# A Fourier mixer and gated FFN on one core: the pair stage in lots of 256 tokens, with seven products in both layers

## The chip, the core and the metric

The kernel runs on one core of one Trainium2 chip. The metric is the device time of one execution in microseconds, the median of several runs. The engines are TensorE (PE in the profile; its weight loads are PEld), VectorE (DVE), ScalarE (ACT), GpSimd (POOL) and SyncE (SP), which here only issues DMAs. Each engine works through its own queue in order and waits on semaphores for the others.

## What is computed

```python
# x: 8 x 3008 x 256;  w_gate, w_val: 256 x 1536;  w_out: 1536 x 256;  all float32
X = np.fft.rfft(x, axis=1)
Y = X @ (w_r + 1j * w_i) + (b_r + 1j * b_i)      # real and imaginary part
Y = sign(Y) * max(abs(Y) - 0.01, 0)              # on each part
y = np.fft.irfft(Y, n=3008, axis=1).reshape(24064, 256)
gate = 1 / (1 + np.exp(-(y @ w_gate)))
out = (gate * (y @ w_val)) @ w_out
```

## The kernel before

A float32 operand is split in two parts, high and low (`float32r`): the high part is a rounded copy that ScalarE writes, the low part is what VectorE (or GpSimd) finds by subtracting it. A product of two split operands is three matmuls: high x high, high x low, low x high.

The first stage (about 1006 us of the span) does the Fourier transforms of all eight batches by matmuls, the mixing between them, and, woven between these, the FFN of the first 9 x 512 tokens (`ffn1`, `ffn2`). The mixed tokens beyond these are written to DRAM (`yd`). Beside it GpSimd forms sums and differences of weight tiles (`make_t`, `t1` to `t4`), stores them (`td`), and SyncE's queue loads them back near the end of the stage (`load_t`, `load_t1`). The hidden width of 1536 is NF = 12 tiles of 128; two tiles (f0, f1) make one of NH = 6 column pairs `fp`.

The second stage is the pair stage, on the remaining 19456 tokens: 19 pairs of two lots of HW = 512 tokens. In the first layer, for each `fp` and for each of i = 0 (gate) and i = 1 (value), a 2 x 2 block problem stands: two hidden tiles x two lots, summed over the two halves of the 256 channels. It is done with seven products instead of eight. The token-side operands are a11, a12, a21, a22 (a lot's half of the channels) and their sums s1 to s4, which GpSimd forms and ScalarE and its helpers split once per pair (`operand`, `split`, at the places of `PREP_AT`). The product list is

```
1: a11 b11   2: a12 b21   3: s4 b22   4: a22 t4   5: s1 t1   6: s2 t2   7: s3 t3
```

Each product is three matmuls 512 wide, all of them in line L714. `half(k)` issues one half step (one `fp`, one i): product 1 into PSUM bank a, 6 into b, 5 into c, 7 into d; ScalarE copies bank a to SBUF (u, L739), VectorE adds u + b (L743), + c (L745), + d (L747); then products 2, 3 and 4 are added on top in banks a, c and d, and VectorE adds u to c (L768) and d (L774). So the sums of products are formed in SBUF by VectorE. The gate's four results pass the sigmoid on ScalarE, the value's are multiplied by them (L753, L764, L779 on VectorE, L772 on GpSimd), and the four hidden blocks are split (`high` L661, `low` L665). `second(n, j)` is the second layer: plain, 2 lots x 2 output tiles x 3 matmuls for one hidden tile, 12 matmuls 512 wide (L689 to L691), added up in four banks over all 12 hidden tiles and then copied out by ScalarE (L671). It is issued one to two half steps behind the first layer. So one half step is 21 + 12 matmuls 512 wide, and there are 19 x 6 x 2 = 228 half steps. The stage's instruction order is written out by hand (`manual_schedule`): each engine runs its instructions in the order of these calls.

Of the kernel before, what the change touches and what calls it, by code (L numbers as in the profile page):

```python
# [25 lines left out]
NPL = 9  # L26
HW = 512
# [3 lines left out]
NCB, NTMP, NHP = 10, 9, 12  # L31
# [78 lines left out]
def tile_fft_mix_ffn(ctx: ExitStack, tc, x, w_r, w_i, b_r, b_i, w_one, w_out, mf, mi, mis, fa, fb, mf0, fa0, out):  # L110
# [334 lines left out]
    BEHIND = 3  # L445
# [133 lines left out]
    def make_t(fp, i):  # L579
# [4 lines left out]
        for k, f in enumerate((f0, f1)):  # L584
            g.tensor_add(b[:, k], w1h[:, f, i], w1l[:, f, i])
# [35 lines left out]
    def operand(p, name):  # L621

        y = held["y", p]
        a11, a21, a12, a22 = y[:, 0, 0], y[:, 0, 1], y[:, 1, 0], y[:, 1, 1]
        g = nc.gpsimd
        if name == "s1":
            held["s", p] = p4.tile([P, HW], F32, name="sop", bufs=1)
            g.tensor_add(held["s", p], a21, a22)
        elif name == "s2":
            g.tensor_sub(held["s", p], held["s", p], a11)  # L630
        elif name == "s3":
            g.tensor_sub(a21, a11, a21)
        elif name == "s4":
            g.tensor_sub(held["s", p], a12, held["s", p])
        held["op", p, name] = {"a11": a11, "a12": a12, "a22": a22, "s3": a21}.get(name, held.get(("s", p)))

    def split(p, name, sub_):
        v = held.pop(("op", p, name))
        t = p4.tile([P, 2, HW], F32R, tag="xop", bufs=NCB, name=name)
        nc.scalar.copy(t[:, 0], v)  # L640
        sub_(t[:, 1], v, t[:, 0])
        xs[p][name] = t

    PREP = ("a11", "s1", "s2", "s3", "a12", "s4", "a22")

    PREP_AT = ((2, 2), (3, 4), (5, 6), (7, 11), (8, 11), (9, 11), (9, 11))

    def tmp(name):
        return p5.tile([P, HW], F32, tag="tmp", bufs=NTMP, name=name)

    gates, hq, po = {}, {}, {}
    after_m1, before_sums, before_second, after_gate = [], [], [], []

    def run(todo):
        for t in todo:
            t()
        todo.clear()

    def high(n, j, s, h):
        hq[n, j, s] = [p5.tile([P, HW], F32R, tag="hp", bufs=NHP, name=t) for t in ("hh", "hl")]  # L660
        nc.scalar.copy(hq[n, j, s][0], h)  # L661

    def low(n, j, s, h, sub_):
        hh, hl = hq[n, j, s]
        sub_(hl, h, hh)  # L665

    def put(o, to, last=False):
        ot = tmp("ot_last") if last else p5.tile([P, HW], F32, name="ot2", bufs=3)

        def todo():  # L670
            nc.scalar.copy(ot, o)  # L671
            nc.sync.dma_start(to, ot)
        return todo

    def second(n, j):

        if not 0 <= n < NPR * NH:
            return
        p, fp = divmod(n, NH)
        f = 2 * fp + j  # L680
        if f == 0:
            po[p] = [[bank("po", "l2", L2_BANKS)[:, :HW] for _ in range(CT)],
                     [psg.tile([P, 512], F32, tag="po2", bufs=CT, name="po2")[:, :HW] for _ in range(CT)]]
        for s in range(2):
            hh, hl = hq.pop((n, j, s))
            for ct in range(CT):
                o = po[p][s][ct]
                wh, wl = (w2[:, f, v, ct * P:(ct + 1) * P] for v in range(2))
                nc.tensor.matmul(o, wh, hh, start=(f == 0), stop=False)  # L689
                nc.tensor.matmul(o, wl, hh, start=False, stop=False)  # L690
                nc.tensor.matmul(o, wh, hl, start=False, stop=(f == NF - 1))  # L691
        if f == NF - 1:
            for s, os in enumerate(po.pop(p)):
                for ct, o in enumerate(os):
                    at = T0 + (2 * p + s) * HW
                    todo = put(o, out[ct * P:(ct + 1) * P, at:at + HW], p == NPR - 1 and s == ct == 1)

                    if s and ct:
                        after_gate.append(todo)
                    else:  # L700
                        todo()

    banks = {}

    def products(k):
        n, i = divmod(k, 2)
        p, fp = divmod(n, NH)
        x, w = xs[p], weights(fp, i)

        def product(o, xn, wn, more=False):  # L710

            (xh, xl), (wh, wl) = (x[xn][:, 0], x[xn][:, 1]), w[wn]
            for l, r in ((wh, xh), (wh, xl), (wl, xh)):
                nc.tensor.matmul(o, l, r, start=not more and l is wh and r is xh, stop=l is wl, skip_group_check=more)  # L714

        return product

    def open_banks(k):
        banks[k] = [psg.tile([P, 512], F32, tag="l1", bufs=4, name=t)[:, :HW] for t in ("pa1", "pb1", "pc1", "pd1")]

    def half(k, extra):

        n, i = divmod(k, 2)
        product = products(k)
        add, mul = nc.vector.tensor_add, nc.vector.tensor_mul
        if k not in banks:
            open_banks(k)
            early = False
        else:
            early = True  # L730
        a, b, c, d = banks.pop(k)

        def product1(*args):
            if not early:
                product(*args)

        u, v = tmp("u"), tmp("v")
        product1(a, "a11", "b11")
        nc.scalar.copy(u, a)  # L739
        run(before_sums)  # L740
        run(after_m1)
        product1(b, "s2", "t2")
        add(u, u, b)  # L743
        product1(c, "s1", "t1")
        add(v, u, c)  # L745
        product1(d, "s3", "t3")
        add(v, v, d)  # L747
        if i == 0:
            g11 = tmp("g11")
            nc.scalar.activation(v, v, AF.Sigmoid)  # L750
        else:
            g11, g12, g21, g22 = gates.pop(n)
            mul(v, g22, v)  # L753
            high(n, 1, 1, v)
            low(n, 1, 1, v, sub)
        run(before_second)
        extra()
        second(n - 1 - (i == 0), 1 - i)
        product(a, "a12", "b21", more=True)
        if i == 0:  # L760
            nc.scalar.activation(g11, a, AF.Sigmoid)
            run(after_gate)
        else:
            mul(g11, g11, a)  # L764
            high(n, 0, 0, g11)
        product(c, "s4", "b22", more=True)
        c12 = tmp("c12")
        add(c12, u, c)  # L768
        if i == 0:
# [406 lines left out]
```

## Time and profile before

| | us |
|---|---|
| median of the runs (lowest to highest of 3) | 2721.54 (2719.38 to 2722.66) |
| span of the profiled execution | 2719.1 |
| PE busy | 2697.9 (99%) |
| DVE busy | 2039.4 (75%) |
| ACT busy | 1350.9 (50%) |
| POOL busy | 722.6 (27%) |

The span is that of one profiled execution, from the first to the last instruction; the runs are timed without the profile, and their median stands 2.4 us above it. The granted TensorE clock is 0.997 on the mean. A line of a timeline gives the start and the length in us, the engine, the line of the kernel, the operation, output<-input by the program's names, the shape, and the count when several were merged; in brackets stands the idle time before it and who ended it. A line of the groups gives the count, the busy time in us, the mean in ns, and the idle time before with its releasers. A matmul's length is its whole passage, and matmuls overlap, so that their rate is read from their starts.

### The profile page before, as it was taken

The page shows a single profiled execution, that of the slowest core. Times are in us where ns is not written, and L with a number is a line of the kernel's source. Part 1 is how long each engine was busy: PE and PEld are TensorE (multiplying, and loading weights), DVE is VectorE, ACT ScalarE, POOL GpSimd, SP SyncE. Part 2 cuts the span into 40 slices and gives each one's busy share as a digit, 9 for nine tenths or more (in the row PEclk, how much of TensorE's full clock was granted, in tenths as well). Part 3 has the DMA queues.
Part 4 walks back from the last instruction along what each step waited for, and adds up shares of the span by engine and source line. Part 5 has one row for each costly group of instructions (what it writes and reads, how often), then busy time and mean ns, then how long its engine had stood idle before and what let it go on. Part 6 is the DMA issues. An engine that isn't in the chain of part 4 may idle for free.

```text
span 2719.1 us, 45261 instructions
## 1 busy us (share of the span) xinstructions
PE 2697.9 (99%) x17364; PEld 2235.9 (82%) x17364; DVE 2039.4 (75%) x3012; ACT 1350.9 (50%) x2373; POOL 722.6 (27%) x665
## 2 busy tenths in 40 slices
PE   9999999999999999999999999999999999999999
PEld 6668888888899788888888888888888888888887
DVE  5777787768777348778777777778777877777776
ACT  4766565565555444444444444444444444444443
POOL 0231020215000003333343333333333333333321
PEclk9999999999999999999999999999999999999999
DMA  9887654777555750000000000000000000000000
GB/s 292 260 248 205 182 159 148 222 203 218 151 167 148 201 166 9 32 32 16 16 31 32 24 8 32 31 32 1 32 32 32 8 24 32 32 16 16 32 16 16
DMA packets 170552, 241.48 MB, mean 89 GB/s; under 512 B 17184, under 2 KB 127648, under 8 KB 170336
## 3 DMA queue, kind: packets, MB, share of 16 engines
q1 hardware_dynamic: 160176, 216.75, 26.6%
q0 software_dynamic: 9904, 21.77, 2.5%
q8 instruction: 137, 2.24, 0.4%
q14 instruction: 79, 0.65, 0.1%
q10 hardware_dynamic: 256, 0.07, 0.0%
HBM read 134.19 MB, written 104.33 MB: 88 GB/s over the span
## 4 chain that ended last, share of the span: by engine, by line
PE 95%; DMA 2%; DVE 1%; ACT 1%; issue 0%; SPq 0%; POOL 0%; ACTq 0%; DVEq 0%
PE pa L714 11%; PE pc L714 11%; PE pd L714 11%; PE po L690 8%; PE po L691 8%; PE po L689 8%; PE pm L306 6%; PE pb L714 6%; PE pb L273 3%; PE pia L389 2%; PE pg L453 2%; PE pg L454 2%; PE pg L455 2%; PE po L481 2%; PE pv L453 2%; PE pv L454 2%
## 5 line engine op out<-in xcount | busy, mean ns | idle before, releaser
L772 POOL TENSOR_TENSOR c<-c,c 128x512 f32<-128x512 f32 x114 | 148.2, 1300 | 779.7 <-DVE c L768 597.7
L691 PE MATMUL po<-hl,w 128*128 128x512 f32 x912 | 354.8, 389 | 0.0
L690 PE MATMUL po<-hh,w 128*128 128x512 f32 x912 | 354.8, 389 | 0.0
L689 PE MATMUL po<-hh,w 128*128 128x512 f32 x912 | 354.8, 389 | 0.0
L714 PE MATMUL pa<-a,w1h 128*128 128x512 f32 x912 | 280.9, 389 | 0.0
L714 PE MATMUL pc<-s,w1h 128*128 128x512 f32 x912 | 280.9, 389 | 0.0
L768 DVE TENSOR_TENSOR c<-u,pc 128x512 f32<-128x512 f32 x228 | 156.6, 687 | 90.2 <-PE pc L714 84.3
L743 DVE TENSOR_TENSOR u<-u,pb 128x512 f32<-128x512 f32 x228 | 155.4, 681 | 91.7 <-PE pb L714 60.5
L661 ACT CAST hh<-v 128x512 fp32r<-128x512 f32 x114 | 70.7, 620 | 306.1 <-DVE v L753 306.1
L665 POOL TENSOR_TENSOR hl<-c,hh 128x512 fp32r<-128x512 f32 x114 | 151.9, 1332 | 186.0 <-ACT hh L661 186.0
L714 PEld LDWEIGHTS pa<-a,w1h 128*128 128x128 f32 x912 | 171.1, 188 | 35.9 <-DVE sg L461 0.4
L714 PEld LDWEIGHTS pc<-s,w1h 128*128 128x128 f32 x912 | 171.1, 188 | 35.8 <-DVE v L745 0.2
L689 PEld LDWEIGHTS po<-hh,w 128*128 128x128 f32 x912 | 171.2, 188 | 35.6
L690 PEld LDWEIGHTS po<-hh,w 128*128 128x128 f32 x912 | 171.2, 188 | 35.5
L691 PEld LDWEIGHTS po<-hl,w 128*128 128x128 f32 x912 | 171.2, 188 | 35.5
L306 PE MATMUL pm<-w_sb,xsh 128*128 128x256 f32 x1008 | 184.3, 285 | 1.3 <-ACT xsh L289 1.3
L714 PE MATMUL pc<-s,w1l 128*128 128x512 f32 x456 | 177.4, 389 | 0.0
L714 PE MATMUL pa<-a,w1l 128*128 128x512 f32 x456 | 177.4, 389 | 0.0
L745 DVE TENSOR_TENSOR v<-u,pc 128x512 f32<-128x512 f32 x228 | 156.8, 688 | 24.5 <-DVE u L743 0.9
L774 DVE TENSOR_TENSOR u<-u,pd 128x512 f32<-128x512 f32 x228 | 156.8, 688 | 24.5 <-DVE c L768 0.9
L747 DVE TENSOR_TENSOR v<-v,pd 128x512 f32<-128x512 f32 x228 | 156.8, 688 | 24.1 <-DVE v L745 0.5
L739 ACT COPY u<-pa 128x512 f32<-128x512 f32 x228 | 133.7, 586 | 69.5 <-PE pa L714 69.0
(182 smaller groups left out, 6605.8 us busy)
## 6 DMA issues: line engine op xcount, KB each, us to landing
zf<-zd SPq DMA_DIRECT2D x96, 256.0 KB, 3.5
vf<-vd SPq DMA_DIRECT2D x128, 192.0 KB, 3.9
out_dram<-ot SPq DMA_DIRECT2D x93, 256.0 KB, 2.2
vd<-vz SPq DMA_DIRECT2D x85, 256.0 KB, 2.9
ypair<-yd SPq DMA_DIRECT2D x19, 1024.0 KB, 4.9
yd<-yf SPq DMA_DIRECT2D x103, 188.0 KB, 3.4
xf<-in_x_dram SPq DMA_DIRECT2D x80, 192.0 KB, 4.4
zd<-xf SPq DMA_DIRECT2D x80, 192.0 KB, 2.9
```

The lines of the kernel that those rows point to most:

```text
L306: nc.tensor.matmul(o, l, r, start=(i == 0), stop=(i == len(mms) - 1))
L665: sub_(hl, h, hh)
L689: nc.tensor.matmul(o, wh, hh, start=(f == 0), stop=False)
L690: nc.tensor.matmul(o, wl, hh, start=False, stop=False)
L691: nc.tensor.matmul(o, wh, hl, start=False, stop=(f == NF - 1))
L714: nc.tensor.matmul(o, l, r, start=not more and l is wh and r is xh, stop=l is wl, skip_group_check=more)
L743: add(u, u, b)
L745: add(v, u, c)
L747: add(v, v, d)
L768: add(c12, u, c)
L772: nc.gpsimd.tensor_mul(c12, g12, c12)
L774: add(u, u, d)
```

## The change

The pair stage runs 38 pairs of two lots of 256 tokens. One step, `slot(k)`, is one `fp` with gate and value together: each first-layer bank holds the gate in its first 256 columns and the value in the other 256, so the seven products are 7 x 2 x 3 = 42 matmuls 256 wide. The sums of products are formed in PSUM: ScalarE copies bank a (product 1) into bank b, products 6 and 3 are added there by TensorE; after product 6 ScalarE copies bank b into bank d, where 7 and 4 are added (`seed`). A matmul at the stage's start marks banks b and d as written, so that the later ones add to what ScalarE put there. Product 5 is copied to SBUF (`take_m5`) and VectorE adds it to banks b and d for the second column (`column2`).

The second layer takes seven products too: GpSimd forms sums of the hidden blocks (`hsum`), three splits per step (`hi` on ScalarE, `lo` on VectorE; X holds h12 and h22, G holds h11 and h11 - h21, S the three sums) feed 7 x 3 = 21 matmuls 256 wide, two steps behind. They accumulate in four banks `acc` over the six steps of a pair. The evictions combine them: ScalarE copies and VectorE adds, five blocks stored plainly or as part of the sum, and one DMA from GpSimd's queue that adds in DRAM (`evict4`). `make_t` forms the combinations of the second layer's weights as a third item of each `fp` (i = 2), 18 items instead of 12; they are loaded by more DMAs (`load_t`, `load_u1`). The next pair's seven operands are prepared in three steps (e = 1, 2, 3 of the pair's six; `prep_steps`), each a sum or two on GpSimd, one hi on ScalarE, one lo on VectorE. In the list below e is the number of the step in its pair; evictions of the pair before fall in e = 1 (`evict1`) and e = 2 (`evict2` to `evict4`).

```diff
-HW = 512
+HW = 256
...
         for k, f in enumerate((f0, f1)):
-            g.tensor_add(b[:, k], w1h[:, f, i], w1l[:, f, i])
+            if i < 2:
+                g.tensor_add(b[:, k], w1h[:, f, i], w1l[:, f, i])
+            else:
+                at = slice(k * P, k * P + P)
+                g.tensor_add(b[:, k], w2[:, f0:f0 + 2, 0, at], w2[:, f0:f0 + 2, 1, at])
...
+    def prep_steps(p, sub_):
...
+        def split(v, names):
...
+            nc.scalar.copy(t[:, 0], v)
+            sub_(t[:, 1], v, t[:, 0])
...
+        return [lambda: sums(1), lambda: split(lambda: held["y", p][:, 1], ("a12", "a22")),
+                lambda: sums(3), lambda: split(lambda: held["y", p][:, 0], ("a11", "s3")),
+                lambda: (sums(2), sums(4)), lambda: split(lambda: held["s", p], ("s1", "s2", "s4"))]
...
+    def first(k, name):
...
+        o, more = {1: (bank_a, False), 2: (bank_a, True), 5: (bank_c, False), 3: (bank_b, True), 6: (bank_b, True),
+                   7: (bank_d, True), 4: (bank_d, True)}[name]
...
+        for i in range(2):
+            wh, wl = weights(fp, i)[wn]
+            for l, r in ((wh, xh), (wh, xl), (wl, xh)):
+                start = not more and i == 0 and l is wh and r is xh
+                nc.tensor.matmul(o[:, i * HW:(i + 1) * HW], l, r, start=start, stop=l is wl, skip_group_check=True)
+
+    ACC = {1: (0, 0), 2: (0, 1), 4: (1, 0), 7: (1, 1), 6: (2, 0), 5: (2, 1), 3: (3, 0)}
...
+    def seed(to, o):
+        nc.scalar.copy(to, o)
+    def take_m5(k):
+        hx[k, "m5"] = p5.tile([P, 2 * HW], F32, name="m5", bufs=1)
+        nc.scalar.copy(hx[k, "m5"], bank_c)
...
+    def column2(k, i):
...
+        o = (bank_b, bank_d)[i]
+        nc.vector.tensor_add(hx[k, "X"][:, :, i], o.rearrange("p (i n) -> p i n", i=2),
+                             hx[k, "m5"].rearrange("p (i n) -> p i n", i=2))
...
+    def hsum(k, i, e):
+        x, g = hx[k, "X"], hx[k, "G"]
+        if i == 1:
+            hx[k, "S"] = p5.tile([P, 3, HW], F32, name="hs", bufs=2)
+            e.tensor_add(hx[k, "S"][:, 0], g[:, 1], x[:, 0, 1])
+        elif i == 2:
+            e.tensor_sub(hx[k, "S"][:, 1], hx[k, "S"][:, 0], g[:, 0])
+        elif i == 3:
+            e.tensor_sub(g[:, 1], g[:, 0], g[:, 1])
         else:
+            e.tensor_sub(hx[k, "S"][:, 2], x[:, 0, 0], hx[k, "S"][:, 1])
...
+    def evict2(p):
+        ev, acc = held["ev", p], accs[p]
+        nc.vector.tensor_add(ev[:, 5], acc[2][:, :HW], ev[:, 0])
+        nc.vector.tensor_add(ev[:, 6], acc[1][:, HW:], ev[:, 5])
+        for ct, lot, i in (0, 1, 6), (1, 0, 5), (1, 1, 6):
+            nc.sync.dma_start(out_of(p)[:, ct, lot * HW:(lot + 1) * HW], ev[:, i])
+        nc.scalar.copy(ev[:, 2], acc[1][:, :HW])
+
+    def evict3(p):
+        ev, acc = held["ev", p], accs[p]
+        nc.scalar.copy(ev[:, 4], acc[2][:, HW:])
+        nc.vector.tensor_add(ev[:, 3], acc[3][:, :HW], ev[:, 4])
+
+    def evict4(p):
+        nc.gpsimd.dma_start(out_of(p), held["ev", p][:, 1:5].rearrange("p (t a) n -> p t (a n)", t=CT), accum_op=ALU.add)
...
+    def slot(k):
+
+        v, g = nc.vector, nc.gpsimd
+        live, before = k < NU, 0 < k <= NU
+        p, e = divmod(k, NH)
+        q = k - 2
+        ends = q >= 0 and q % NH == NH - 1
+        begins = q > 0 and q % NH == 0
...
+        if live and k:
+            first(k, 1)
+            seed(bank_b, bank_a)
+            first(k, 5)
+        if begins:
+            evict2(qp - 1)
+        if before:
+            for i in 1, 3, 2, 4:
+                hsum(k - 1, i, v if last else g)
+            hi(k - 1, "X")
+            lo(k - 1, "X")
...
+        second(q, 1, 2)
+        if live and k:
+            first(k, 6)
+            seed(bank_d, bank_b)
+        if before:
+            hi(k - 1, "G")
+            lo(k - 1, "G")
+        if live:
+            if k:
+                first(k, 2)
+            gate11(k)
+            h11(k)
+            take_m5(k)
+        if begins:
+            evict3(qp - 1)
+            evict4(qp - 1)
+        second(q, 4)
+        if ends:
+            evict1(qp)
+        if live:
+            if k:
+                first(k, 7)
+                first(k, 3)
+            column2(k, 1)
+            column2(k, 0)
+        if before:
+            hi(k - 1, "S")
+            lo(k - 1, "S")
+        if steps and 0 < e < 4:
+            steps[2 * e - 2]()
+            steps[2 * e - 1]()
+        second(q, 7, 6, 5)
+        if live:
+            gate2(k)
+            first(k, 4)
+            gate21(k)
+            h2(k)
+            h21(k)
+        second(q, 3)
```

`gate2` is the sigmoid of X's gate half, 512 wide; `gate11` and `gate21` are sigmoids of 256 columns from banks a and d; `h2`, `h11` and `h21` multiply by the value (512, 256 and 256 wide, on VectorE); `hi` and `lo` are 512 wide for X and G and 768 for S. In the stage's last two steps no first layer is left, the sums run on VectorE, and `evict_last` combines the last pair.

More of the change, by code (lines that the diff above doesn't have):

```diff
@@ L637, in split @@
[L637 to L673, printed above, removed]
@@ L675, in second @@
-    def second(n, j):
-        if not 0 <= n < NPR * NH:
-            return
[L679 to L728, printed above, removed]
-        else:
[L730 to L769, printed above, removed]
-            nc.scalar.activation(c12, c12, AF.Sigmoid)
-        else:
-            nc.gpsimd.tensor_mul(c12, g12, c12)
-        product(d, "a22", "t4", more=True)
-        add(u, u, d)
-        if i == 0:
-            after_m1.append(lambda: nc.scalar.activation(u, u, AF.Sigmoid))
-            gates[n] = g11, c12, u, v
-        else:
-            before_sums.append(lambda: mul(u, g21, u))
-            after_m1.append(lambda: high(n, 0, 1, u))
-            after_m1.append(lambda: high(n, 1, 0, c12))
-            after_m1.append(lambda: low(n, 1, 0, c12, nc.gpsimd.tensor_sub))
-            before_second.append(lambda: low(n, 0, 0, g11, sub))
-            before_second.append(lambda: low(n, 0, 1, u, sub))
@@ new lines, in tile_fft_mix_ffn, with second @@
+    ACC = {1: (0, 0), 2: (0, 1), 4: (1, 0), 7: (1, 1), 6: (2, 0), 5: (2, 1), 3: (3, 0)}
+    def second(k, *names):
+        if not 0 <= k < NU:
+            return
+        p, fp = divmod(k, NH)
+        if p not in accs:
+            accs[p] = [psg.tile([P, 512], F32, tag="acc", bufs=2, name="acc") for _ in range(2)]
+        w = weights2(fp)
+        for name in names:
+            b, h = ACC[name]
+            if b == len(accs[p]):
+                accs[p] += [bank("acc2", "l2", L2_BANKS) for _ in range(2)]
+            o = accs[p][b][:, h * HW:(h + 1) * HW]
+            xn, wn = PRODUCTS[name]
+            (hh, hl), (wh, wl) = hop[k].pop(xn), w[wn]
+            for l, r in ((wh, hh), (wh, hl), (wl, hh)):
+                start = fp == 0 and name in (1, 4, 6, 3) and l is wh and r is hh
+                nc.tensor.matmul(o, l, r, start=start, stop=l is wl, skip_group_check=True)
@@ L1071, in tile_fft_mix_ffn @@
     p4 = None
-    ts = [(fp, i) for fp in range(NH) for i in range(2)]
+    ts = [(fp, i) for fp in range(NH) for i in range(3)]
     for j in range(NF, len(ffn)):
@@ L1099, in tile_fft_mix_ffn @@
             if prep and f > 2:
-                operand(0, prep[0])
-                split(0, prep.pop(0), sub)
+                prep.pop(0)()
     while to_load:
@@ L1104, in tile_fft_mix_ffn @@
     while prep:
-        operand(0, prep[0])
-        split(0, prep.pop(0), sub)
+        prep.pop(0)()
+    for fp in range(NH - 1):
+        load_u1(fp)
     psfs.close()
     psg = ctx.enter_context(tc.tile_pool(name="psg", bufs=1, space=bass.MemoryType.PSUM, reuse_waits="tile"))
-    open_banks(0)
-    first_product = products(0)
-    a, b, c, d = banks[0]
-    for o, xn, wn in (a, "a11", "b11"), (d, "s3", "t3"), (b, "s2", "t2"), (c, "s1", "t1"):
-        first_product(o, xn, wn)
+    bank_a, bank_c, bank_b, bank_d = (psg.tile([P, 512], F32, name=t) for t in ("pa1", "pc1", "pb1", "pd1"))
+    ones = th[:, 0, 0].rearrange("p a n -> p (a n)")
+    for o in bank_b, bank_d:
+        nc.tensor.matmul(o[:, :384], th[:, 0, 0, 0], ones, start=True, stop=True, skip_group_check=True)
+        nc.tensor.matmul(o[:, 384:], th[:, 0, 0, 0], ones[:, :128], start=False, stop=True, skip_group_check=True)
+    first(0, 1)
+    seed(bank_b, bank_a)
+    first(0, 5)
+    first(0, 6)
+    seed(bank_d, bank_b)
+    first(0, 2)
+    first(0, 7)
+    first(0, 3)
     p3s.close()
```

166 lines of the change are left out of this document (120 added, 46 removed).

## The prediction

> **What bounds the kernel now.** I read the page's first part and its chain, then the timelines of single engines in the pair stage, then the groups with their shapes kept apart.
>
> ```profile
> PE 2697.9 (99%) x17364; PEld 2235.9 (82%) x17364; DVE 2039.4 (75%) x3012; ACT 1350.9 (50%) x2373; POOL 722.6 (27%) x665
> PE 95%; DMA 2%; DVE 1%; ACT 1%; issue 0%; SPq 0%; POOL 0%; ACTq 0%; DVEq 0%
> L689 PE MATMUL po<-hh,w 128*128 128x512 f32 x912 | 354.8, 389 | 0.0
> 1999.74 0.39 PE L689 MATMUL po<-hh,w 128*128 128x512 f32 x1
> ...
> 2006.54 0.39 PE L689 MATMUL po<-hh,w 128*128 128x512 f32 x1
> ...
> 2714.88 0.39 PE L691 MATMUL po<-hl,w 128*128 128x512 f32 x1
> 2715.30 0.58 ACT L671 COPY ot_last<-po 128x512 f32<-128x512 f32 x1
> ```
>
> The chain is PE and the matmul group has no idle time before it: TensorE never waits in the pair stage. Between the two L689 rows lie 30 matmuls (9 of the second layer, 21 of the first): 6.80 / 30 = 0.2267 us each; the 0.389 in the group is one matmul's whole passage. L689 runs 912 = 228 x 4 times, and each of the 228 half steps issues 21 + 12 matmuls: 7524, or 1705.7 us. So before, every other engine hides behind 7.48 us of TensorE per half step. The question is whether that still holds when TensorE has less to do and waits on chains inside one step.
>
> **TensorE's part.** After, there are 38 pairs x 6 steps = 228 steps of 42 + 21 matmuls, all 256 wide. Such matmuls stand in the Fourier stage:
>
> ```profile
> 191.71 0.39 PE L306 MATMUL pm<-w_sb,xsh 128*128 128x256 f32 x2
> ...
> 192.96 0.28 PE L306 MATMUL pm<-w_sb,xsl 128*128 128x256 f32 x1
> ```
>
> 11 starts in 1.25 us: 0.1136 each, half of a 512-wide one, so the weight load in front of each still hides. At 0.1133, 63 are 7.14 us, a pair (6 steps) 42.84 us against 1705.7 / 38 = 44.89 for the same 512 tokens before: 2.05 us less, 78 us over 38 pairs. That is the whole gain, and stalls of 2.05 us in a pair eat it.
>
> **The other engines' part.** Durations for the new mix:
>
> ```profile
> L739 ACT COPY u<-pa 128x512 f32<-128x512 f32 x228 | 133.7, 586 | 69.5 <-PE pa L714 69.0
> L770 ACT ACTIVATE c<-c 128x512 f32<-128x512 f32 x114 | 72.2, 634 | 75.6 <-DVE c L768 75.4
> L661 ACT CAST hh<-v 128x512 fp32r<-128x512 f32 x114 | 70.7, 620 | 306.1 <-DVE v L753 306.1
> L289 ACT CAST xsh<-xsf 128x768 fp32r<-128x768 f32 x84 | 70.0, 834 | 67.5 <-PE pm L306 36.6 <-DVE xsf L287 29.5 <-PE pi L353 1.3
> L409 ACT COPY carry<-pia 128x248 f32<-128x248 f32 x1 | 0.4, 365 | 0.4 <-DVE ytl L378 0.4
> L745 DVE TENSOR_TENSOR v<-u,pc 128x512 f32<-128x512 f32 x228 | 156.8, 688 | 24.5 <-DVE u L743 0.9
> L665 DVE TENSOR_TENSOR hl<-v,hh 128x512 fp32r<-128x512 f32 x114 | 78.9, 692 | 78.2 <-ACT hh L661 78.2
> L333 DVE TENSOR_TENSOR ys<-pm,bias 128x256 f32<-128x256 f32 x2 | 0.8, 417 | 0.0
> L290 DVE TENSOR_TENSOR xsl<-xsf,xsh x84: 940/958/1515, 185.2 to 880.2; 128x768 fp32r<-128x768 f32 x84
> L585 POOL TENSOR_TENSOR tb<-w1h,w1l x24: 711/740/1300, 364.7 to 652.4; 128x256 f32<-128x256 f32 x24
> ```
>
> ScalarE per step: two seeds 2 x 0.59 (PSUM to PSUM, in no row: lower bound the 0.365 of half the size, upper the 0.634 sigmoid; taken as L739, the same size from PSUM), gate11 and gate21 0.38 each, take_m5 0.59, gate2 0.63, three hi copies 0.62 + 0.62 + 0.83: 5.2 us. VectorE: column2 2 x 0.69, h11 and h21 2 x 0.42, h2 0.69, three lo 0.69 + 0.69 + 0.96: 5.3 us. GpSimd: four hsum at 0.715 (the least of L585, undisturbed): 2.9 us. A pair adds 2.1 of splits and 1.3 of evictions on ScalarE, 2.3 and 1.3 on VectorE, four sums and one accumulating DMA (about 3.4) on GpSimd: sums of 35, 35 and 21 us of 42.84. No engine is full. The steps' order is the matter, and one thing makes it longer:
>
> ```profile
> 1509.73 0.69 DVE L768 TENSOR_TENSOR c<-u,pc 128x512 f32<-128x512 f32 x1
> 1510.53 0.69 DVE L774 TENSOR_TENSOR u<-u,pd 128x512 f32<-128x512 f32 x1
> 1511.25 1.15 DVE L779 TENSOR_TENSOR u<-u 128x512 f32<-128x512 f32 x1
> 1514.51 0.99 DVE L665 TENSOR_TENSOR hl<-g,hh 128x512 fp32r<-128x512 f32 x1
> 1515.42 1.78 DVE L665 TENSOR_TENSOR hl<-u,hh 128x512 fp32r<-128x512 f32 x1
> 1510.57 1.29 POOL L772 TENSOR_TENSOR c<-c,c 128x512 f32<-128x512 f32 x1 [7.02 <-DVE c L768]
> 1513.66 1.30 POOL L665 TENSOR_TENSOR hl<-c,hh 128x512 fp32r<-128x512 f32 x1 [1.80 <-ACT hh L661]
> 1514.90 1.75 POOL L634 TENSOR_TENSOR sop<-ypair,sop 128x512 f32<-128x512 f32 x1
> 1512.44 0.62 ACT L661 CAST hh<-u 128x512 fp32r<-128x512 f32 x1 [0.77 <-DVE u L779]
> 1512.97 0.61 ACT L661 CAST hh<-c 128x512 fp32r<-128x512 f32 x1
> ```
>
> GpSimd's L772 runs 1510.57 to 1511.86. VectorE's L774, with one operand in PSUM, passes beside it in its usual 0.69. L779, with both operands in SBUF, takes 1.15 and ends 0.54 after L772 does: it waited. GpSimd's L634 takes 1.75 because L665 (1514.51 to 1515.50) is in its way, and the next L665 takes 1.78 because L634 is in its. So a VectorE instruction with two SBUF operands and a GpSimd one exclude each other, for all but their first 0.14 us. Here those are h2 and the three lo on one side, all sums on the other. The same rows give the hand-overs: VectorE to ScalarE 0.04 (1512.40 to 1512.44), VectorE to GpSimd 0.15 (1510.42 to 1510.57), and a follower on the same engine starts 0.09 ahead of the end (1512.97). TensorE's price for a stop:
>
> ```profile
> 700.56 0.69 DVE L319 TENSOR_TENSOR yl<-yc,yh 128x512 fp32r<-128x512 f32 x1 [0.68 <-ACT yh L318]
> 701.31 0.38 PE L352 MATMUL pi<-yl,mi_sb 128*128 128x256 f32 x1 [0.34 <-DVE yl L319]
> 701.53 0.28 PE L353 MATMUL pi<-yh,mi_sb 128*128 128x256 f32 x1
> ```
>
> It restarts 0.06 after the release and its second matmul comes 0.22 after the first, not 0.11: 0.17 on top of each wait.
>
> **One light step (no split, no eviction)**, laid end to end from these durations, us from its first matmul: TensorE runs products 1 and 5 and second-layer 1, 2 to 2.04, product 6 to 2.72, product 2 to 3.40, second-layer 4 to 3.74, products 7 and 3 to 5.10, second-layer 7, 6, 5 to 6.12, product 4, second-layer 3 to 7.14. ScalarE: seed of bank b 0.88, hi of X from 1.39 to 2.01, seed of bank d 2.92 to 3.52 (product 6 plus its passage), hi of G to 4.05, gate11 to 4.34, take_m5 to 4.84. GpSimd can begin after h21 of the step before (1.22): hsum 1.36 to 2.08, the second asked at 2.11 but behind lo of X (2.04 to 2.73) until 3.31, the third to 3.97, the fourth to 4.72. VectorE's lo of G asks at 4.08, just behind that fourth sum, and ends 5.27 instead of 4.77; h11 5.60, column2 for bank d 6.20. Product 4 overwrites bank d and wanted 6.12: it starts 6.25 and pays the restart, 0.24 in all. If lo of G asks ahead of the sum, the stall is zero; I take 0.24 for e = 5, 0 and 1 (the step with e = 1 has its extra work behind column2).
>
> **The heavy steps.** e = 2: h21 of e = 1 came 0.6 late (the lo of the split, 0.69, stands ahead of h2 in VectorE's queue), so the second sum ends 3.93, hi of G 4.59, gate11 and take_m5 5.38, then the eviction's copy 5.66 and its add 6.11 stand ahead of column2, which ends 6.71: stall 0.59 + 0.17 = 0.76. e = 3: GpSimd has six sums in a row, from 2.1 to 7.3 with two waits behind lo instructions (0.9); the split's hi waits for the last, 0.83, its lo 0.96, and behind that h2 and h21 end at 10.1. Its own stall is about 0.27 (column2 as in a light step). e = 4 therefore starts its sums at 2.8: second sum 4.65, hi of G 5.30, take_m5 6.10, column2 6.96 against 6.12: 0.84 + 0.17 = 1.0.
>
> A pair: 3 x 0.24 + 0.76 + 0.27 + 1.0 = 2.75 us of stall against 2.05 gained: +0.7, or +27 us over 38 pairs.
>
> **The ends and the first stage.** Before, the last matmul starts at 2714.88 and its only follower is one copy and one DMA. After, two empty steps drain the last sums, splits and second layer, then eight adds: the third sum to the last lo about 5, 42 matmuls partly beside it, adds 2.5: +3. At the start the six products run through two seeds one behind the other: +1. The six more weight combinations on GpSimd lie beside the first FFN chunks; the twelve of before lengthened VectorE's L470 by 0.03 on the mean (the first line is for the transfers below):
>
> ```profile
> DMA  9887654777555750000000000000000000000000
> L470 DVE TENSOR_TENSOR hl<-sg,hh 128x512 fp32r<-128x512 f32 x105 | 75.5, 719 | 41.0 <-ACT hh L469 40.1
> ```
>
> Against L665's 0.692 for the same subtraction, 105 x 0.027 = 2.8 us of VectorE time, half again 1.4, mostly off TensorE's path: +1, and not above +3 if all of it showed. The more loads of combined weights, the half-size ypair loads and the output DMAs go at nothing: the page's slices show DMA at 0 tenths for the whole pair stage (slice 16 on); if a load of ypair came late, the split of e = 1 has two steps to spare. The accumulating DMA is the last instruction of GpSimd in e = 2 but one sum, and queued behind it is only that sum.
>
> Sum on the profiled execution: 2719.1 + 27 + 3 + 1 + 1 = 2751 of span; the median of the runs, 2721.5, stands 2.4 above the span: about 2754.
>
> **Rivals.** (1) Faster: the chains keep ahead of TensorE. Its place is the light step's lo of G and the six sums of e = 3; if 256-wide sums and the lo instructions did not exclude each other, column2 would be through at 5.7 in every step and only e = 2's eviction would stall (0.4 to 0.5): 43.3 us a pair, -60 + 5, 2666. For it: no engine's sum is over 82% of 42.84, and the rows show exclusion between 512-wide instructions. Against: L779, and L585's 1.300 at most for a 256-wide sum that needs 0.711. It decides at 1.9 us of stall a pair. If half of the heavy steps' delay is absorbed, 44.1 us a pair, 2697. (2) No change: the exclusion costs only in e = 2 and e = 4 (1.76) and the other steps slip into the order without a stall: 44.65 a pair, -9 + 5, 2718. For it: a hundredth or two decides who asks first. (3) Slower still: in e = 2 lo of X falls behind a sum too, so that e = 3 starts late and stalls 0.8, and the seeds take their upper end, 0.05 more in front of the light steps' chain, so that these stall 0.35: 46.45 a pair, +59 + 5, 2786. For it: VectorE, ScalarE and GpSimd all stand in that chain, and each delay of one is handed on. (4) The weight load does not hide behind 256-wide matmuls over a whole stage: against it stand the 11 starts above; 0.115 instead of 0.1133 would be +24, though then the chains stall less. (5) The eviction's readers wait for each other. In e = 2 ScalarE copies one half of bank acc 1 and VectorE adds from the other half, behind another add (0.42 each, from 1.73 on). If the copy may not start before that add ends at 2.6, it ends at 3.0 instead of 1.8, hi of X at 3.6, the seed of d at 4.1, and product 7, wanted at 3.74, stalls too: 0.37 more a pair, +14 us, 2768. No row of before has two engines at one bank, for or against. The Trainium skill's page "PSUM — Partial Sum Buffer" (section "PSUM bank collisions raise a hardware error") has a rule by which (5) holds: two engines at one bank and quadrant at once collide, even where both only read, so they are to be kept apart; by it the sum would be 2768 and not 2754, and nothing here shows it yet.
>
> **How the numbers follow.** Forecast (2754) 0.36; (3) and (4) 0.16; (5) 0.14; no change (2) 0.11; half absorbed (2697) 0.12; chains ahead (2666) 0.11. A measurement of this kernel tells about 0.2% (5 us) from no change. Faster 0.23, same 0.11, slower 0.66. The forecast's own range is 2738 to 2786; as both signs hold much, the range leaves out only 2666 below and (3) with (5) above: 2690 to 2800.
>
> **What would show it.** Right: PE no longer 99% busy, idle time before product 4's matmuls released by VectorE's column2, before product 7 in e = 2 by the seed; starts 0.1133 apart elsewhere; lo of G about 1.2 us rather than 0.69 in many steps; sums above 0.715; pairs of 45 to 46.5 us. Wrong: product 4 without a wait, lo instructions at 0.69, or seeds far from 0.59.

## The result and the profile after

The changed kernel takes 2845.77 us (median of 4 runs, 2843.69 to 2846.35) against 2722.05 (2719.38 to 2722.66): a ratio of 1.0451 [1.0436, 1.0466], 124 us slower. The profiled execution spans 2844.4 us at a granted clock of 0.995, 125.3 us more than before. Two places carry it. The pair stage's first matmul comes at 1025.66 us, before at 1005.82: 19.8 us later. The pair stage itself then takes 105.4 us more.

From the page of the changed kernel: the engines' shares, its chain, and the groups that matter.

```profile
PE 2744.1 (96%) x24208; PEld 2508.0 (88%) x24208; DVE 2059.9 (72%) x3240; ACT 1757.1 (62%) x3302; POOL 1153.9 (41%) x1399
PE 50%; DVE 25%; POOL 12%; ACT 6%; issue 4%; DMA 3%; SPq 0%; DVEq 0%; ACTq 0%; POOLq 0%
L772 DVE TENSOR_TENSOR hpG<-gh,hpG 128x512 fp32r<-128x512 f32 x228 | 241.5, 1059 | 258.1 <-ACT hpG L768 258.1
L684 PE MATMUL pd<-a,th 128*128 128x256 f32 x1824 | 366.5, 294 | 50.3 <-DVE xg L736 41.6
L772 DVE TENSOR_TENSOR hpX<-xg,hpX 128x512 fp32r<-128x512 f32 x228 | 197.9, 868 | 157.1 <-ACT hpX L768 157.1
L755 POOL TENSOR_TENSOR gh<-gh 128x256 f32<-128x256 f32 x227 | 247.0, 1088 | 17.8
L707 ACT COPY pd<-pb 128x512 f32<-128x512 f32 x228 | 130.7, 573 | 135.0 <-ACT hpX L768 91.8
L707 ACT COPY pb<-pa 128x512 f32<-128x512 f32 x228 | 131.3, 576 | 87.5 <-PE pa L684 87.5
```

The chain was TensorE for 95% and is now TensorE for 50%, with VectorE and GpSimd for 37%: the chains between the engines set the pace. Low parts of G take 1.06 us on the mean where 0.69 is the undisturbed length, and GpSimd's second sum of a step (L755) 1.09 where 0.715 is: both wait for each other, as the prediction had it.

From the view of the waits, the rows that bear on the prediction (who waits for whom: total us, count, longest):

```profile
ACT a L662 <- POOL ypair L654: 100.3, 36, 3.3
PEld pd L684 <- DVE xg L736: 88.7, 205, 1.2
ACT ev L793 <- DVE ev L790: 42.1, 37, 1.2
PE pd L684 <- DVE xg L736: 41.6, 109, 1.0
PEld pb L684 <- ACT pb L707: 30.2, 55, 1.2
PE pb L684 <- ACT pb L707: 20.1, 36, 1.0
```

The second and fourth are the ones that the prediction named: product 4 waits for column2. The first, third, fifth and sixth are not in its sum.

Worked out from the starts of product 1 (the distance from one step's first matmul to the next step's, mean over the 36 full pairs), in us:

```
              e=0    e=1    e=2    e=3    e=4    e=5    pair
predicted     7.38   7.38   7.90   7.41   8.14   7.38   45.59
after         7.52   7.52   8.28   8.59   8.24   7.52   47.67
```

A pair took 44.89 before, so the 36 full pairs cost (47.67 - 44.89) x 36 = 100.1 us more. The first pair has no evictions in it and the last no splits; they take about 45.3 us each, 0.9 more together, and the rest of the 105.4, about 4 us, is the ends of the stage. The miss of 2.08 a pair is 1.18 in e = 3, 0.38 in e = 2, 0.42 in the three light steps together and 0.10 in e = 4.

What happens between e = 2 and e = 3, from the timelines of single engines (step e = 3 begins at 1618.25):

```profile
1616.80 1.19 POOL L801 DMA_DIRECT2D out_dram<-ev  x1 [1.57 <-DVE ev L798]
1617.58 1.52 POOL L654 TENSOR_TENSOR ypair<-ypair 128x256 f32<-128x256 f32 x1
...
1617.56 0.94 DVE L772 TENSOR_TENSOR hpS<-hs,hpS 128x768 fp32r<-128x768 f32 x1
...
1619.12 0.62 ACT L662 CAST a<-ypair 128x512 fp32r<-128x512 f32 x1 [2.86 <-POOL ypair L654]
1619.65 0.63 ACT L714 ACTIVATE xg<-xg 128x512 f32<-128x512 f32 x1
...
1621.09 0.50 PE L684 MATMUL pb<-s,th 128*128 128x256 f32 x2 [0.62 <-ACT pb L707]
```

The accumulating DMA (`evict4`) waits for the eviction's last add and then holds GpSimd for 1.2 us. The split's one sum (L654) stands behind it, so it comes up just as lo of S begins, and the two are in each other's way: it takes 1.52 us, not 0.7, and ends at 1619.10. ScalarE's split (L662) has waited 2.86 us for it, and behind that split in ScalarE's queue stands the sigmoid `gate2` (L714) of e = 2, on which h2, h21 and all of e = 3 hang. TensorE waits 0.62 us, until 1621.09, because the seed of bank b comes too late.

### The profile page after: what moved, and what is told of

It is laid out like the page before. It is cut to its first block, busy times and chain, and to the rows that moved or that the text cites. A ratio compares the mean times of both kernels' runs of the same rounds, so it can differ in the third digit from the quotient of the medians.

```text
span 2844.4 us, 60508 instructions
## 1 busy us (share of the span) xinstructions
PE 2744.1 (96%) x24208; PEld 2508.0 (88%) x24208; DVE 2059.9 (72%) x3240; ACT 1757.1 (62%) x3302; POOL 1153.9 (41%) x1399
## 4 chain that ended last, share of the span: by engine, by line
PE 50%; DVE 25%; POOL 12%; ACT 6%; issue 4%; DMA 3%; SPq 0%; DVEq 0%; ACTq 0%; POOLq 0%
PE pd L684 6%; PE acc L704 6%; PE pa L684 5%; PE pb L684 5%; PE pm L307 5%; DVE xg L736 4%; POOL gh L755 3%; PE pc L684 3%; DVE xg L744 2%; PE pb L274 2%; DVE gh L722 2%; PE pia L390 2%; DVE hpG L772 2%; POOL hs L751 2%; DVE hpS L772 2%
## 5 line engine op out<-in xcount | busy, mean ns | idle before, releaser
L772 DVE TENSOR_TENSOR hpG<-gh,hpG 128x512 fp32r<-128x512 f32 x228 | 241.5, 1059 | 258.1 <-ACT hpG L768 258.1
L684 PE MATMUL pd<-a,th 128*128 128x256 f32 x1824 | 366.5, 294 | 50.3 <-DVE xg L736 41.6
L684 PEld LDWEIGHTS pd<-a,th 128*128 128x128 f32 x1824 | 275.6, 188 | 101.4 <-DVE xg L736 88.7
L684 PE MATMUL pa<-a,w1h 128*128 128x256 f32 x1824 | 336.7, 278 | 0.0
L755 POOL TENSOR_TENSOR gh<-gh 128x256 f32<-128x256 f32 x227 | 247.0, 1088 | 17.8
L684 PE MATMUL pd<-a,tl 128*128 128x256 f32 x912 | 253.8, 278 | 0.0
L684 PE MATMUL pa<-a,w1l 128*128 128x256 f32 x912 | 252.7, 277 | 0.0
L772 DVE TENSOR_TENSOR hpS<-hs,hpS 128x768 fp32r<-128x768 f32 x228 | 244.6, 1073 | 0.0
L704 PE MATMUL acc<-hpS,w 128*128 128x256 f32 x1368 | 234.3, 280 | 0.0
L757 POOL TENSOR_TENSOR hs<-xg,hs 128x256 f32<-128x256 f32 x227 | 214.2, 944 | 17.8
L714 ACT ACTIVATE xg<-xg 128x512 f32<-128x512 f32 x228 | 144.0, 632 | 116.4 <-DVE xg L736 112.7
```

What stands on the lines that cost most here:

```text
L684: nc.tensor.matmul(o[:, i * HW:(i + 1) * HW], l, r, start=start, stop=l is wl, skip_group_check=True)
L704: nc.tensor.matmul(o, l, r, start=start, stop=l is wl, skip_group_check=True)
L714: nc.scalar.activation(o, o, AF.Sigmoid)
L755: e.tensor_sub(g[:, 1], g[:, 0], g[:, 1])
L757: e.tensor_sub(hx[k, "S"][:, 2], x[:, 0, 0], hx[k, "S"][:, 1])
L772: sub(t[:, 1], parts_of(k, what), t[:, 0])
```

## Experiments

All are edits of the changed kernel, and all ratios are to the kernel before, run again beside each group of experiments (2720.61, 2721.9 and 2722.19 us). The means of their steps, worked out as above, with the start of the pair stage and the median time:

```
                e=0   e=1   e=2   e=3   e=4   e=5   pair   start    time
after           7.52  7.52  8.28  8.59  8.24  7.52  47.67  1025.7  2845.8
f1_ulate        7.53  7.52  8.29  8.65  8.24  7.53  47.75  1009.7  2833.8
e1_dma_late     7.53  7.53  8.28  7.33  8.19  7.53  46.39  1021.0  2795.8
e2_copy_first   7.53  7.52  7.79  8.99  8.12  7.53  47.48  1024.1  2837.1
e3_memset       7.20  7.20  7.62  8.18  7.20  7.21  44.61  1019.9  2728.3
e5_pause        7.27  7.28  8.20  7.32  8.21  7.36  45.64  1023.2  2765.4
e6_split_late   7.53  7.54  8.07  7.36  7.55  7.52  45.57  1026.1  2768.3
v1              7.52  7.53  7.41  7.29  7.30  7.29  44.34  1011.9  2709.6
v1_pause        7.23  7.32  7.41  7.26  7.20  7.28  43.70  1012.1  2685.2
```

**The DMA in GpSimd's queue (e1_dma_late).** `evict4` is issued behind the split's sum instead of ahead of it.

```diff
         evict3(qp - 1)
-        evict4(qp - 1)
 ...
         steps[2 * e - 1]()
+    if begins:
+        evict4(qp - 1)
```

> The changed kernel, with the accumulating DMA (evict4) issued on GpSimd behind the sum for the split of e = 2 instead of ahead of it. Theory: that DMA holds GpSimd 1.2 us and makes the split's sum, the split, h2 and h21 late, so that e = 3 stalls 1.4 us instead of 0.3; the step e = 3 falls from 8.59 to 7.5 us, the others stay, and the time falls by about 40 us, to 2805. Rival: e = 3 is late through its own six sums in a row or through the eviction's adds on VectorE; then e = 3 stays above 8.3 and the time above 2835.

Measured: 2795.81 us (2794.38 to 2799.48), ratio 1.0277 [1.0259, 1.0294]. e = 3 falls by 1.25 us to 7.33, next to the prediction's 7.41, and no other step moves by more than 0.05. 1.28 in each of 36 full pairs is 46 us of the 50 that the time fell; the rest is the first stage, which this edit does not touch and which in this run ended 4.7 us earlier. The place of one DMA in one queue is the largest part of the miss.

**The two readers of bank acc 1 (e2_copy_first).** In `evict2` ScalarE's copy is issued ahead of VectorE's two adds.

```diff
     ev, acc = held["ev", p], accs[p]
+    nc.scalar.copy(ev[:, 2], acc[1][:, :HW])
     nc.vector.tensor_add(ev[:, 5], acc[2][:, :HW], ev[:, 0])
 ...
-    nc.scalar.copy(ev[:, 2], acc[1][:, :HW])
```

> The changed kernel, with the eviction's ScalarE copy from bank acc 1 issued ahead of the two VectorE adds, so that it does not wait for the add from the same bank. Theory: the copy's wait (1.1 us in the trace) puts hi of X and the seed of d behind, 0.37 us in e = 2; the time falls by 14 us, to 2832, and e = 2 takes 7.9 instead of 8.28 us. Rival: e = 2 is bound by column2 behind the eviction's adds, as in the prediction's own sum, and nothing falls: 2843 to 2846.

In the changed kernel's timeline the copy starts when the add on the other half of the bank ends:

```profile
1612.12 0.42 DVE L790 TENSOR_TENSOR ev<-acc,ev 128x256 f32<-128x256 f32 x1
1612.58 0.37 ACT L793 COPY ev<-acc 128x256 f32<-128x256 f32 x1 [1.13 <-DVE ev L790]
```

With the copy first, e = 2 falls from 8.28 to 7.79, about as expected, so the wait and its price are shown. But the time falls only to 2837.09 us (2832.54 to 2840.16), ratio 1.0424 [1.0408, 1.0439], since the mean of e = 3 grows from 8.59 to 8.99. That growth is six pairs in a row. In the other 30, e = 3 takes 8.27 to 9.12 us, as in the changed kernel (8.28 to 9.05); in these six it takes 9.92 to 11.40. In all six, the last of the eviction's three stores lands 7.3 to 7.7 us into e = 2, elsewhere at 5.3 to 6.5, and the accumulating DMA starts only behind that landing. The split's sum behind it is late in turn, and TensorE stops in e = 3 for 1.83 to 2.31 us. Of one of these pairs a row of GpSimd's timeline, a row of TensorE's, and a row of the windows (window, its length, then busy time and count of PE, PEld, DVE, ACT and POOL, the granted clock, the DMA share, GB/s):

```profile
2131.42 1.20 POOL L801 DMA_DIRECT2D out_dram<-ev  x1 [2.06 <-DMA out_dram<-ev]
...
2135.38 0.50 PE L684 MATMUL pb<-s,th 128*128 128x256 f32 x2 [1.83 <-ACT pb L707]
...
2136.70:2140.00 3.30, 3.30 (x18) 3.30 (x17) 1.98 (x4) 2.01 (x5) 3.22 (x4) 0.50 0.01 2
```

After four of the six stops the granted clock fell to 0.50, as in the last row; after the other two it stayed at 1.00. Why the store lands late in just these six pairs is open.

**Do sums and low parts exclude each other (e3_memset).** GpSimd's four sums of a step are left out, and in each one's place GpSimd writes a constant to a tile of 512 or 768 columns.

```diff
+        if e is nc.gpsimd:
 ...
+            e.memset(g if i in (1, 3) else hx[k, "S"], 0.25)
+            return
```

> The changed kernel, with the four sums of hidden blocks per step replaced on GpSimd by four memsets of 512 or 768 columns (the sums are left out): GpSimd is still busy in the same places, between the same waits, but reads nothing from SBUF. Theory: VectorE's subtractions and GpSimd's sums exclude each other, and that makes the light steps 7.52 instead of 7.14 us and part of the heavy ones; without it the light steps are 7.14 to 7.2, lo of G 0.69 us, a pair 45.0 instead of 47.7, and the time falls by about 95 us, to 2750. Rival: the mere place of GpSimd's work in the chain costs the time, exclusion or not; then the light steps stay at 7.4 or more and the time above 2820.

Measured: 2728.3 us (2726.29 to 2730.57), ratio 1.0025 [1.0015, 1.0034]. The groups:

```profile
L752 POOL MEMSET hs<- 128x768 f32 x454 | 337.1, 743 | 13.1
L752 POOL MEMSET gh<- 128x512 f32 x454 | 239.2, 527 | 918.0 <-DVE gh L729 905.0
L777 DVE TENSOR_TENSOR hpG<-gh,hpG 128x512 fp32r<-128x512 f32 x228 | 159.7, 701 | 244.1 <-ACT hpG L773 244.1
L777 DVE TENSOR_TENSOR hpX<-xg,hpX 128x512 fp32r<-128x512 f32 x228 | 158.0, 693 | 188.1 <-ACT hpX L773 188.1
```

GpSimd stays busy for 2 x 0.527 + 2 x 0.743 = 2.5 us a step in the same places, but reads nothing, and the low parts drop from 1.06 and 0.87 to 0.70 and 0.69. The light steps go from 7.52 to 7.20. That speaks for the exclusion as the cause of the light steps' stall of 0.32. The four writes are together 0.3 us shorter than four undisturbed sums (4 x 0.715), so that this run alone does not rule out the length of GpSimd's queue; the next one does, where GpSimd has more to do. The time is 22 us below the 2750 expected: e = 4 falls to 7.20 too, and the pair stage began 5.8 us earlier than the changed kernel's. e = 2 and e = 3, where the eviction's wait and the DMA stay, still take 7.62 and 8.18.

**Who asks first (e5_pause).** On top of e1_dma_late, one small write of 160 columns to a tile that nobody reads is put between GpSimd's third and fourth sum of each step.

```diff
+                if i == 4 and not last:
+                    g.memset(p5.tile([P, 160], F32, name="pause", bufs=1), 0.0)
                 hsum(k - 1, i, v if last else g)
```

> e1_dma_late (2795.8 us) with one more GpSimd instruction per step: a memset of 160 columns that nobody reads, about 0.24 us, between the third and the fourth sum of hidden blocks. Theory: in a light step the fourth sum asks for the shared way to SBUF about 0.05 us ahead of lo of G, which then waits a whole sum; with the pause lo of G comes first, takes 0.69 us, and the light steps fall from 7.53 to 7.2 us although GpSimd has more to do: three light steps and part of e = 2, a pair 45.3 instead of 46.4, the time 2755. Rival: the light steps are bound by the length of the chain through GpSimd, or by the same total of excluded time wherever it falls; then the pause adds, and the time is 2800 or more.

Measured: 2765.43 us (2762.44 to 2769.22), ratio 1.0155 [1.0138, 1.0172], 30 us less than e1_dma_late. Of this kernel the group of the write and a light step (e = 1, from 1624.63); behind it the changed kernel's (e = 1, from 1602.43):

```profile
L841 POOL MEMSET pause<- 128x160 f32 x227 | 52.1, 230 | 0.0
...
1628.60 0.22 POOL L841 MEMSET pause<- 128x160 f32 x1
1628.79 1.26 POOL L757 TENSOR_TENSOR hs<-xg,hs 128x256 f32<-128x256 f32 x1
...
1628.75 0.69 DVE L772 TENSOR_TENSOR hpG<-gh,hpG 128x512 fp32r<-128x512 f32 x1 [1.39 <-ACT hpG L768]
```

```profile
1606.53 0.74 POOL L757 TENSOR_TENSOR hs<-xg,hs 128x256 f32<-128x256 f32 x1
...
1606.55 1.27 DVE L772 TENSOR_TENSOR hpG<-gh,hpG 128x512 fp32r<-128x512 f32 x1 [1.39 <-ACT hpG L768]
```

In the changed kernel the fourth sum starts 0.02 us ahead of lo of G, and lo of G takes 1.27. With 0.22 us more work in GpSimd's queue the order turns round: lo of G takes 0.69 and the sum 1.26, and the step takes 7.20. That happens in 55 of the 108 light steps of the full pairs, and in e1_dma_late in none; those 55 take 7.20 us each, the others 7.31 to 7.61. (In e = 3 and e = 4, lo of G comes first without the pause, in e1_dma_late too, and these steps do not change.) "A hundredth or two decides who asks first" was the prediction's sentence for its rival (2); it fell on the dear side.

**The split in ScalarE's queue (e6_split_late).** On top of e1_dma_late, a split's hi and lo are issued behind h21 of the step instead of ahead of `gate2`.

```diff
-    if steps and 0 < e < 4:
-        steps[2 * e - 2]()
-        steps[2 * e - 1]()
+    if steps:
+        for i in {1: (0,), 2: (2,), 3: (4,)}.get(e, ()):
+            steps[i]()
 ...
     h21(k)
+    if steps and e in {1: 1, 2: 3, 3: 5}:
+        steps[{1: 1, 2: 3, 3: 5}[e]]()
```

> e1_dma_late (2795.8 us) with the splits of the next pair (hi and lo, in e = 1, 2, 3) issued behind h21, not ahead of gate2 and h2; their sums on GpSimd stay where they are. Theory: the split's lo stands ahead of h2 and h21 in VectorE's queue, and in e = 3 behind six sums; behind h21 it delays no chain. e = 2 falls from 8.28 to 8.0, e = 4 from 8.19 to 7.65 (what stays is GpSimd's two more sums), the time by 40 us, to 2755. Rival: VectorE and ScalarE lack the time anyway, so that the split delays the next step's lo of X as much as it did h2: 2785 to 2800.

Measured: 2768.33 us (2763.43 to 2770.34), ratio 1.0167 [1.0152, 1.0182]. e = 4 falls from 8.19 to 7.55 and e = 2 from 8.28 to 8.07: what made e = 4 long was the split of e = 3 ahead of `gate2` and h2, as the prediction had laid it out (its hi on ScalarE and its lo on VectorE were moved together, so which of the two weighs more is not shown). The exclusion has a part in it: in e3_memset, where the split stands as in the changed kernel, e = 4 takes 7.20. The pair stage gets 30 us shorter, of which 27 show, since it began 5 us later than e1_dma_late's.

**The loads in the first stage (f1_ulate).** The twelve loads of the second layer's weight combinations leave `load_t` and are issued behind the loop.

```diff
 def load_t(fp):
-    for v, (t, u) in enumerate(((th, uh), (tl, ul))):
+    for v, t in enumerate((th, tl)):
 ...
+for fp in range(NH):
+    load_u(fp)
 for fp in range(NH - 1):
     load_u1(fp)
```

> The changed kernel, with the loads of the second layer's combined weights (uh, ul) taken out of the last chunk of the first stage and put behind its loop. Theory: these 12 loads change the order of the inverse transform's matmuls (groups of 64 alternating between two halves of the array become groups of 32), and that is most of the 20 us by which the pair stage starts later; with the loads behind the loop the pair stage starts at about 1010 us instead of 1025.7 and the time falls by about 15 us, to 2831. Rival: the six more weight combinations on GpSimd (about 7 us each) hold VectorE up there; then the start stays above 1020 us and the time above 2840.

Measured: 2833.84 us (2833.22 to 2837.02), ratio 1.0415 [1.04, 1.0431]: 12 us less. The pair stage begins at 1009.73 where 1010 was expected. The first stage's order is not written out by hand, and with these loads in it it came out otherwise. The inverse transform's last matmuls run in groups of 64 before and in f1_ulate; in the changed kernel ten groups of 32 and one of 128 stand among those of 64. Rows of TensorE's timeline, of before, of after, and of f1_ulate, for the last two with a row of the windows:

```profile
925.12 1.15 PE L389 MATMUL pia<-fb_sb,vf 48*64 48x47 f32 x64
```

```profile
927.62 1.13 PE L390 MATMUL pia<-fb_sb,vf 48*64 48x47 f32 x32
929.58 1.13 PE L390 MATMUL pia<-fb_sb,vf 48*64 48x47 f32 x32
...
941.94 1.14 PE L390 MATMUL pia<-fb_sb,vf 48*64 48x47 f32 x32 [1.26 <-DMA vf<-vd]
...
935.00:957.00 22.00, 20.74 (x283) 16.45 (x279) 4.41 (x7) 7.20 (x16) 0.00 (x0) 0.84 0.85 237
```

```profile
927.33 1.15 PE L390 MATMUL pia<-fb_sb,vf 48*64 48x47 f32 x64
...
935.00:957.00 22.00, 21.27 (x326) 16.95 (x326) 5.55 (x9) 9.33 (x18) 0.00 (x0) 1.00 0.84 235
```

A group of 32 takes 1.13 us, one of 64 takes 1.15: half the work in the same time. Added up over the groups, each to the start of the next instruction, the last 1024 of these matmuls take 26.2 us in the changed kernel, 19.0 in f1_ulate and 18.2 before. From the first of the 1024 to the pair stage it is 92.2 us before and 91.2 to 92.2 in the four kernels that have these loads behind the loop, 101.5 to 102.1 in the five others of the experiments, and 105.4 in the changed kernel. So the loads' place costs about 10 us, and the groups are about 7 of them. The changed kernel's 3.4 more go with the granted clock, 0.84 in the window shown; none of the five others has a lowered clock there, so they are no part of the change's price. Nor is the wait of 1.26 us for a DMA: before has one of 1.50 us at 920.60.

**Both queues mended at once (v1, v1_pause).** v1 joins f1_ulate, e1_dma_late and e2_copy_first, issues the three splits' hi and lo behind h21, in e = 1, 2 and 4, and the sums for each one step ahead, in e = 0, 1 and 3. v1_pause adds the small write.

```diff
+        for i in {0: (0,), 1: (2,), 3: (4,)}.get(e, ()):
+            steps[i]()
 ...
+    if steps and e in {1: 1, 2: 3, 4: 5}:
+        steps[{1: 1, 2: 3, 4: 5}[e]]()
```

> All together: the late loads of uh and ul (f1_ulate), the eviction's copy ahead of its adds (e2_copy_first), the accumulating DMA late (e1_dma_late), the splits behind h21 (e6_split_late) but each one step later than now for the last (e = 1, 2, 4), and each sum for them on GpSimd one step ahead of its split (e = 0, 1, 3). Theory: the heavy steps' stalls come from these orders alone; then e = 3, 4, 5 take 7.2, e = 0, 1 still 7.45 to 7.5, e = 2 7.4: 44.0 us a pair, and with the first stage back the time is 2692. Rival: the work of VectorE and ScalarE (35 us each of 43, beside the exclusion) has no room, and the stalls only move to other steps: above 2740.

> v1 with the pause of e5_pause. Theory: light steps at 7.2 as well, 43.4 us a pair, 2672. Rival: as for e5_pause; not faster than v1.

Measured: v1 2709.59 us (2707.13 to 2713.67), ratio 0.9955 [0.994, 0.997]; v1_pause 2685.19 (2684.83 to 2686.69), ratio 0.9865 [0.985, 0.988]. v1_pause beats both kernels: 37 us under the one before, 161 under the change. Its page:

```profile
PE 2657.8 (99%) x24208; PEld 2479.8 (92%) x24208; DVE 2011.9 (75%) x3240; ACT 1772.9 (66%) x3302; POOL 1265.6 (47%) x1626
L776 DVE TENSOR_TENSOR hpG<-gh,hpG 128x512 fp32r<-128x512 f32 x228 | 177.4, 778 | 251.4 <-ACT hpG L772 251.4
```

TensorE is back at 99%, lo of G at 0.78. A pair takes 43.70 us: of the 2.05 that the smaller products can bring, 1.19 are kept, x 38 = 45 us, of which 6 go to the first stage and about 4 to the ends of the pair stage. Both kernels missed their expected times by 13 to 18 us. Part of that is the matmuls' rate: the steps without a stop (e = 4 here; e = 0, 1 and 4 in e3_memset) take 7.20 us and not 7.14. Rows of v1_pause without any wait between them:

```profile
1605.43 0.40 PE L688 MATMUL pd<-a,th 128*128 128x256 f32 x2
...
1607.55 0.52 PE L708 MATMUL acc<-hpS,w 128*128 128x256 f32 x3
...
1609.65 0.39 PE L688 MATMUL pc<-s,w1h 128*128 128x256 f32 x2
1610.33 0.50 PE L708 MATMUL acc<-hpG,w 128*128 128x256 f32 x3
```

From the first to the second lie 18 starts in 2.12 us, 0.1178 each; from the third to the fourth 6 in 0.68, 0.1133 each. Some stretches are slower by 4%. The granted clock is 1.00 in both of these; what sets the difference is open.

**The combinations on GpSimd (e7_no_combos).** v1_pause without the six second-layer combinations; the loads fetch a first-layer one in their place.

```diff
-    ts = [(fp, i) for fp in range(NH) for i in range(3)]
+    ts = [(fp, i) for fp in range(NH) for i in range(2)]
```

> v1_pause (2685.2 us) without the six weight combinations of the second layer on GpSimd (left out; the loads stay and fetch a first-layer combination instead). Theory: the 6 us by which the pair stage of v1_pause still starts later than before's (1012.1 against 1005.8 us) are GpSimd's combinations in VectorE's way during the first stage; without them it starts at about 1006 us and the time falls by 6, to 2679. Rival: the start is late for another reason, one chunk of the second layer more ahead of it (1.4 us) and the loads; then it stays at 1010 or more and the time at 2683 or more.

Measured: 2683.26 us (2680.91 to 2684.17), ratio 0.9854 [0.9838, 0.9871]. The pair stage begins at 1007.71, 4.4 earlier, but the time falls by only 1.9, and the intervals of the two ratios overlap. The three other kernels with the loads behind the loop begin it at 1009.7 to 1012.1. So the combinations may cost the first stage 2 to 4 us; it is not settled.

## Why the prediction was right and wrong

**The direction and the mechanism** held. TensorE's matmuls did get cheaper, the chains between the engines took more than that back, product 4 waited for column2 in nearly every step (its weight loads in 205 of 228), and the exclusion between VectorE's low parts and GpSimd's sums is what makes the light steps stall (e3_memset, e5_pause). Rivals (1), chains ahead of TensorE, and (2), no change, fall with that.

**The step that failed** is the sentence "The accumulating DMA is the last instruction of GpSimd in e = 2 but one sum, and queued behind it is only that sum", by which the DMA went at nothing in the path to e = 3. In the sum of GpSimd's work it stood at about 0.5 us (3.4 less four sums of 0.715); the rows of before have DMA issues of 0.54 to 0.74 us on GpSimd (L168, L253, L358), and none that accumulates. The place in the queue was read right. But the DMA first waits 1.57 us for the eviction's last add and then holds GpSimd for 1.2 us, and the one sum behind it is not the end of the line: ScalarE's split waits for it, and `gate2`, and so the whole next step, waits behind the split. e = 3 stalled 1.44 us instead of 0.27; 1.18 in each of 36 full pairs is 42 us of the miss of 92. e1_dma_late gives it back; it takes the DMA's wait and its issue away together and does not part the two.

**Rival (5), the eviction's readers**, was true and was not in the sum. The copy waits 1.13 us for the add. The Trainium skill's page "PSUM — Partial Sum Buffer" (section "PSUM bank collisions raise a hardware error"), by which two engines' accesses to one bank are to be kept apart even where both only read, agrees with this: here the order of the two is kept by a wait. Its price was put at 0.37 a pair; e = 2 missed by 0.38, and turning the two round took 0.49 off that step.

**The light steps** stalled 0.38 instead of 0.24. 0.06 of it is the rate of the matmuls, 7.20 instead of 7.14 for 63 of them: rival (4) in a small form, about 14 us if it holds in all 228 steps. Rival (3) had 0.35 for these steps, but by seeds at their upper end, and these took 0.57. The layout itself, end to end from single durations, was close: lo of G was read as 0.69 plus a wait and came at 1.27, the fourth sum just ahead of it.

**e = 4** was put at 8.14 and came at 8.24, for the reason given: the split of e = 3 ahead of h2, and the exclusion (e6_split_late, e3_memset).

**The first stage** was put at +1, "and not above +3", and came at +19.8. The second term that failed stands here: the loads of combined weights went at nothing, because the page showed DMA at 0 tenths for the pair stage. But these loads are in the first stage, where the same row has 4 to 9 tenths, and with them the transforms' matmuls came out in another order. They cost about 10 us, of which the smaller groups are about 7 (f1_ulate and the three other kernels with the loads behind the loop). 3.4 us more are the lowered clock of that one execution. The other 6.6 us come ahead of the last 1024 inverse matmuls, where the ten changed kernels differ by up to 8 us among themselves; the six combinations may be a part of it (e7_no_combos). The six kernels that have the changed kernel's first stage began the pair stage anywhere from 1019.9 to 1026.1, so single figures of a few us in it prove little.

**Durations**: the seeds took 0.573 and 0.576 where 0.59 was taken, take_m5 0.585. The ends of the pair stage were put at +3 and its beginning at +1; together they came at about 4.

**The rivals' sums**: half of the heavy steps' delay taken off gives 44.6 us a pair by the prediction's own terms, or 43.9 with no stall in the light steps either, and not the 44.1 behind its 2697; the forecast does not rest on it.

## What to carry to other kernels

When work is moved into chains within one step, follow every instruction that is queued behind a long or late one through at least two further queues: "only one sum" stood behind the DMA, but a split stood behind the sum, and the next step behind the split. Where two instructions on different engines exclude each other and nearly tie, the order of asking is worth more than the length of either: 0.2 us of useless work on the engine that may wait gained 30 us. And read the stages beside the change too, where the order isn't written out by hand: twelve loads added there cost about 10 us by the order that they brought about.

## What the runs showed of the hardware

Issuing an accumulating DMA of 512 KB holds GpSimd for 1.197 us; the groups of the changed kernel, with the sum behind it:

```profile
L654 POOL TENSOR_TENSOR ypair<-ypair 128x256 f32<-128x256 f32 x38 | 52.8, 1390 | 0.1
...
L801 POOL DMA_DIRECT2D out_dram<-ev x37 | 44.3, 1197 | 59.5 <-DVE ev L798 55.4 <-DVE xg L736 4.1
```

A GpSimd instruction that only writes doesn't exclude VectorE's subtraction of two SBUF tiles: 0.693 and 0.701 us beside the writes against 0.868 and 1.059 beside the sums. The Trainium skill's page "SBUF — State Buffer" (section "Who interferes with whom") says that such an instruction contends with a GpSimd one that reads SBUF and not with one that only writes it; the runs agree.

A copy by ScalarE from PSUM to PSUM (0.573 and 0.576 us for 512 columns) costs hardly less than one from PSUM to SBUF (0.585). Matmuls 256 wide start 0.1133 to 0.1178 us apart with no wait between them, and what makes the difference is open. In e2_copy_first the granted clock was 0.50 for 3.4 us after a stop of 1.83 us, and again after three others of 2.17 to 2.31 us; after two stops of 1.91 and 2.31 us it stayed at 1.00.
